# Routing order and the fetches of two expert slots in a fused attention and mixture-of-experts kernel

## The chip, the cores and the metric

The kernel runs on one core of one Trainium2 chip, as one program. The metric is device time in microseconds (us), and a kernel's time is the median of its runs. Lower is better.

The engines have the names that the profile gives them: PE is TensorE's matrix product and PEld its loading of weights, DVE is VectorE, ACT is ScalarE, POOL is GpSimd, and SP is SyncE, which here issues most of the transfers.

## The reference

Attention comes first, with two batches of 576 tokens, 8 heads and 64 columns a head. Its result, 1152 tokens of 512 values, goes through a top-1 mixture of 8 experts. An expert takes its tokens in their order up to a capacity of 288, and what comes after that is dropped (its row stays zero).

```python
q_rot, k_rot = rotate(q), rotate(k)
attn = softmax(q_rot @ k_rot.T / sqrt(D))
x = (attn @ v).transpose(0, 2, 1, 3).reshape(1152, 512)

logits = x @ w_gate                    # 8 experts
e = argmax(logits, 1)
gate = softmax(logits)[e]
...
h = maximum(disp[e] @ w1[e], 0)        # 512 -> 1024, up to 288 tokens
y = h @ w2[e]                          # 1024 -> 512
out[token] = gate[token] * y
```

The inputs are drawn at random, and q and k are scaled up by 5.76 and 5.75, so the tokens are spread unevenly over the experts. Worked out on the host with the reference, the first batch gives its experts 0, 0, 0, 18, 0, 452, 106 and 0 tokens, and both batches together 0, 33, 0, 18, 0, 454, 155 and 492.

## The kernel before

**Stages.** The attention works through eight steps, four pairs of heads for batch 0 and then four for batch 1, in an order written out by hand (`ORDER`). While batch 1 is worked on, the routing of batch 0 (`Router.batch(0)`, then `Router.first`) runs in between in small steps on DVE. `first` picks the expert with most tokens in batch 0; that is slot 0, with 288 tokens, and its weights are loaded and its tokens fetched while the attention goes on. It also picks the second expert of batch 0. The first four of slot 0's eight groups of the first product are made at the attention's end (until about 190 us in the trace).

**A slot** is one expert's work. `load` (L912, rows L920 and L923) brings eight tiles of weights, four of w1 and four of w2, on SP's queue. Each tile is split into a rounded high part on ACT (`split_hi`, L932) and a rest on DVE or POOL (`split_lo`, L936), since the matrix product takes rounded operands and three products are summed. `gather_tile` (L906) fetches up to 128 tokens by an indirect transfer on POOL's queue into the tile `xg`; `disp_t` (L950) transposes them on PE, and `disp_h` on ACT (L954) and `disp_l` on DVE (L958) write them to `d`, high part and rest. `gemm1_wide` (L1005) makes one of eight groups of the first product in 12 matmuls, `relu_hi` (ACT, L1030) and `relu_lo` (DVE, L1036 and L1037) put it into `h`. `gemm2` (L1101) makes the second product for 128 tokens in two steps of 12 matmuls or four of 6, `rows_a` (ACT, L1116) scales by the gate, and `scatter` (L1132) writes the rows out on POOL's queue. A slot of 64 tokens has forms of its own (`gemm1_few`, L1056; `ht_copy`, L1060; `ht_transpose`, L1071; `split_tok`, L1079 and L1084; `disp5_h` and `disp5_l`, L962 and L965).

**Buffers.** There are two sets of eight raw weight tiles, used by turns (`raw[0]` for slot 0), and one set of split tiles, so a tile can be split for the next slot only when the slot before has used it, and loaded for the slot after only when it has been split. `xg` is one buffer for all slots, and so are `d`, `d1` and `h`.

**Slot 0's plan.** `first_slot` follows the hand-written list `PLAN`, in which each entry is one step, emitted in that order on its engine (`manual_schedule`). G, RH, RL, M, YA, YD and YS are a group of gemm 1, relu high and rest, gemm 2 (M.2j and M.2j+1 are the two steps for the j-th 128 tokens), scaling, and scatter. SH and SL split slot 0's w2; VH and VL split slot 1's w1. DT, DH and DL transpose slot 1's tokens and write `d`. X fetches the tokens of the next slot, and E makes the register loads. B is one step of the second routing, which is interleaved here: `Router.batch(1)`, then `Router.finish`.

**The second routing.** `batch(1)` sums the logits (the small product LL is L547), finds each token's expert (OH, L572), counts with products (L587), and makes M (L645) and the table of tokens by expert (product L651, result `tab`, L658). Between its steps `order` (L744 to L795) sorts the experts: slot 0's is known, slot 1 is the second expert of batch 0, the rest go by their counts. `finish` (L802 and L806) selects all eight slots' rows of the table by that order, and `tables` (L670 to L687) turns them into the fetch indices `gi`, the scatter indices `si` and the gates. As soon as `gi` is there, slot 1's three tiles of tokens are fetched. Step X of the plan then fetches three tiles of the next slot into the same `xg`.

**The branch.** E.0 copies the 18 numbers of `order` to `after` (L1431), and E.1 loads registers from them. SP loads eight experts' numbers (L1434), and all five engines load eight numbers of the general path (L1436) and the flag (L1437). `If` (L1444) then takes the usual path when the slots' counts stay within `MOST`, here 160, 288, 64 and 64 tokens and none after that. `usual` is straight-line code for the four slots by the list `STEPS`, worked on in the order `SEQUENCE` (1, 3, 2, 4), where slot 2 has 288 tokens and slots 1, 3 and 4 have 160, 64 and 64; the entries have the slot behind the point and carry the letters above, with LD a load, SP a split on POOL, and C and T the copy and the transposition of a small slot. This part isn't bound to the order of the list: a scheduler moves instructions within it. The other path, `slots`, goes through the slots with a jump table each (`later_slot`, `ahead`).

## Time and profile before

| what | value |
|---|---|
| runs | 313.56, 314.19, 316.22 us |
| median | 314.19 us |
| the profiled execution: its own time | 315.87 us |
| its span (first to last instruction) | 314.1 us |
| mean granted clock of TensorE | 0.928 |
| busy: PE, PEld | 282.9 us (90%), 255.1 us (81%) |
| busy: DVE, ACT, POOL | 224.5 us (71%), 194.1 us (62%), 153.2 us (49%) |

A profile shows one execution. In its rows a line number is the line of the kernel that made the instruction, `out<-in` are the program's names for the tiles, and the granted clock is the share of full speed that TensorE was given. A busy share is a mean over stages with different limits: the attention (until 190 us) has DVE and PE both nearly full, the routing stage (190 to about 220) has a long chain of small DVE steps beside PE's work, and in the last 40 us little but PE's work is left. What an edit is worth has to be read in the stage that it touches.

### The profile page before, as it was taken

The page shows a single profiled execution, that of the slowest core. Times are in us where ns is not written, and L with a number is a line of the kernel's source. Part 1 is how long each engine was busy: PE and PEld are TensorE (multiplying, and loading weights), DVE is VectorE, ACT ScalarE, POOL GpSimd, SP SyncE. Part 2 cuts the span into 40 slices and gives each one's busy share as a digit, 9 for nine tenths or more (in the row PEclk, how much of TensorE's full clock was granted, in tenths as well). Part 3 has the DMA queues.
Part 4 walks back from the last instruction along what each step waited for, and adds up shares of the span by engine and source line. Part 5 has one row for each costly group of instructions (what it writes and reads, how often), then busy time and mean ns, then how long its engine had stood idle before and what let it go on. Part 6 is the DMA issues. An engine that isn't in the chain of part 4 may idle for free. (4 is left out here: it accounts for less than half of the span.)

```text
span 314.1 us, 5909 instructions
## 1 busy us (share of the span) xinstructions
PE 282.9 (90%) x1920; PEld 255.1 (81%) x1920; DVE 224.5 (71%) x475; ACT 194.1 (62%) x435; POOL 153.2 (49%) x197
## 2 busy tenths in 40 slices
PE   4699999999999988898999999997976995999990
PEld 2387999999999887897998999865974694998890
DVE  3989779789988999898977829973264548366511
ACT  1158779789888875477899943711435385356541
POOL 4999968959312877905316631166330064100251
PEclk9979999999999999589999999996975699799997
DMA  5576869675643764237987117725586489600020
GB/s 169 144 210 166 189 195 250 162 181 138 167 104 79 181 157 101 47 73 199 341 184 263 40 48 257 269 75 158 198 301 258 154 285 337 231 0 0 2 76 15
DMA packets 36103, 50.29 MB, mean 160 GB/s; under 512 B 10328, under 2 KB 20696, under 8 KB 36064
## 3 DMA queue, kind: packets, MB, share of 16 engines
q1 hardware_dynamic: 34608, 45.61, 49.5%
q0 software_dynamic: 1456, 4.22, 4.2%
q8 instruction: 17, 0.28, 0.4%
q14 instruction: 22, 0.18, 0.2%
HBM read 31.57 MB, written 6.49 MB: 121 GB/s over the span
## 5 line engine op out<-in xcount | busy, mean ns | idle before, releaser
L316 ACT ACTIVATE pe<-sc,mx 128x576 f32<-128x576 f32 x72 | 53.6, 746 | 12.5 <-DVE mx L307 11.8
L307 DVE TENSOR_REDUCE mx<-sc 128x1 f32<-128x576 f32 x72 | 53.8, 751 | 9.2 <-PE sc L303 5.5
L350 DVE TENSOR_TENSOR PTl<-pt,PTh 128x512 fp32r<-128x512 f32 (+1 forms) x80 | 48.8, 630 | 5.6 <-ACT PTh L346 5.1
L346 ACT CAST PTh<-pt 128x512 fp32r<-128x512 f32 (+1 forms) x80 | 42.1, 548 | 12.3 <-PE pt L328 9.9
L328 PE MATMUL pt<-cst,pe 128*128 128x128 f32 x288 | 43.9, 282 | 0.9 <-ACT pe L316 0.4
L303 PE MATMUL sc<-d,QS 128*128 128x288 f32 x224 | 43.9, 321 | 0.7 <-ACT pe L316 0.7
L1132 POOL DMA_INDIRECT out_dram<-y,si x10 | 11.2, 1115 | 61.4 <-DVE y L1125 35.8
L936 DVE TENSOR_TENSOR w2l<-raw,w2h 128x1024 fp32r<-128x1024 f32 x18 | 23.2, 1300 | 20.5 <-ACT w2h L932 20.3
L328 PEld LDWEIGHTS pt<-cst,pe 128*128 128x128 f32 x288 | 34.7, 145 | 3.4 <-ACT pe L316 1.0
L391 PE MATMUL acc<-PTh,VV 128*128 128x288 f32 x128 | 36.9, 311 | 0.2
L391 PE MATMUL acc<-PTl,VV 128*128 128x288 f32 x128 | 34.9, 295 | 0.0
L303 PEld LDWEIGHTS sc<-d,QS 128*128 128x128 f32 x224 | 33.2, 197 | 1.7 <-ACT pe L316 1.6
L1101 PE MATMUL sc<-w2h,h 128*128 128x512 f32 (+2 forms) x80 | 31.3, 436 | 2.6 <-DVE h L1037 2.6
L932 ACT CAST w2h<-raw 128x1024 fp32r<-128x1024 f32 x20 | 20.7, 1048 | 11.7 <-issue 6.3
L211 POOL TENSOR_TENSOR raw<-raw,cst 128x640 f32<-128x640 f32 (+1 forms) x16 | 23.2, 1449 | 6.9 <-PE pt L243 3.7
L1005 PE MATMUL sc<-d,w1h 128*128 128x288 f32 (+1 forms) x120 | 25.9, 314 | 0.0
L936 DVE TENSOR_TENSOR w1l<-raw,w1h 128x1024 fp32r<-128x1024 f32 x15 | 17.7, 1220 | 11.3 <-ACT w1h L932 11.3
L391 PEld LDWEIGHTS acc<-PTh,VV 128*128 128x128 f32 x128 | 24.2, 189 | 0.9 <-ACT accs L395 0.4
L906 POOL DMA_INDIRECT xg<-x_dram,gi x14 | 16.3, 1167 | 16.3 <-DVE h L1037 7.0
L391 PEld LDWEIGHTS acc<-PTl,VV 128*128 128x128 f32 x128 | 24.1, 188 | 0.0
L1101 PEld LDWEIGHTS sc<-w2h,h 128*128 128x128 f32 (+1 forms) x80 | 16.7, 209 | 7.7 <-ACT h L1030 3.3
L1101 PE MATMUL sc<-w2l,h 128*128 128x512 f32 (+2 forms) x56 | 22.2, 407 | 0.0
(235 smaller groups left out, 685.4 us busy)
## 6 DMA issues: line engine op xcount, KB each, us to landing
raw<-in_moe_w_dram SPq DMA_DIRECT2D x40, 512.0 KB, 5.8
d<-HH SPq DMA_DIRECT2D x28, 144.0 KB, 2.7
d<-LL SPq DMA_DIRECT2D x28, 144.0 KB, 2.4
out_dram<-raw SPq DMA_DIRECT2D x9, 256.0 KB, 3.0
raw<-in_k_dram SPq DMA_DIRECT2D x8, 256.0 KB, 3.0
raw<-in_q_dram SPq DMA_DIRECT2D x8, 256.0 KB, 2.8
raw<-in_v_dram SPq DMA_DIRECT2D x8, 256.0 KB, 3.0
x_dram<-xm SPq DMA_DIRECT2D x8, 256.0 KB
```

The source lines that it names most:

```text
L211: eng.tensor_tensor(R, x, cos.to_broadcast(full), ALU.mult)
L303: nc.tensor.matmul(o, st["QS", j][:, qc], st[k, j][:, cs], start=(x == 0), stop=(x == 1))
L307: self.nc.vector.tensor_reduce(mx, self.st[n]["sc", u][:, :, 0:288], AX.XY, ALU.max, negate=True)
L316: self.nc.scalar.activation(pe.rearrange("p (a c) -> p a c", a=2), st["sc", u][:, :, 0:288], AF.Exp, bias=st["mx", u], accum_out=self.sums ...
L328: nc.tensor.transpose(ps[:, c * P:(c + 1) * P], pe[:, 64 + c * P:64 + (c + 1) * P], self.ident)
L346: self.nc.scalar.copy(h, p)
L350: self.nc.vector.tensor_tensor(l, p, h.bitcast(F32), ALU.subtract)
L391: nc.tensor.matmul(acc[:, 0:288], w, m, start=(c == 1 and x == 0), stop=(c == 0))
L932: self.nc.scalar.copy(self.W[u][0], self.raw[q][u])
L936: eng.tensor_tensor(lo, self.raw[q][u], hi.bitcast(F32), ALU.subtract)
L1005: self.nc.tensor.matmul(ps[:, 0:n], w, self.d[:, c, a, 0:n], start=(c == 0 and x == 0), stop=(c == 3 and x == 2))
L1101: self.nc.tensor.matmul(o[0:r, 0:w], a, b, start=(c == 0 and x == 0), stop=(c == 7 and x == len(prods) - 1))
```

## The change

It has these parts.

- `first` also finds the third expert of batch 0. The second and third expert of batch 0 are slots 1 and 2, and their tables and fetches no longer need the sort. The usual path now holds when the slots have at most 160, 64, 288 and 64 tokens, and works on them in the order 1, 2, 3, 4.
- `slots12` selects the table rows of slots 1 and 2 alone, and slot 1's fetch has two tiles (`SECOND`: 128 and 32 tokens) in place of three. `order` runs behind that in steps O of the plan, and selects the rows of slots 3 and 4 at its end. The rows of slots 5 to 8, the kinds of the slots and the numbers of the jump tables are made in `others`, and the remaining tokens fetched in `whole`, both behind the branch on the general path.
- Before the branch one register, the flag, is loaded on every engine (L1467), and two experts' numbers on SP (L1471). The copy `after` is gone.
- Slot 2's weights are asked for in slot 0's plan (LDB), and its 64 tokens are fetched there in one tile (X.0). Slot 1's weights are asked for step by step (LDA). Slot 0's splits SG.7, VG.2 and VG.3 are on POOL.
- The step M.3 of slot 0's gemm 2 stands ahead of the transposes DT. Two groups of gemm 1 (G.7 and G.6) stand ahead of the routing's first product, and three small products of the routing that were on POOL (`val`, `jh`) are on DVE.
- Slot 4's tokens have a tile of their own, `xg4`.

The diff, cut:

```diff
     def batch(self, b, bank):
...
-        order = self.order() if b else iter(())
...
-        next(order, None)
...
-        G.tensor_tensor(val[:, :, 1], sm, keep, ALU.mult)
-        G.tensor_tensor(val[:, :, 0], self.const[:, C_PID + 5 * b:C_PID + 5 * b + 5], keep, ALU.mult)
+        V.tensor_tensor(val[:, :, 1], sm, keep, ALU.mult)
+        V.tensor_tensor(val[:, :, 0], self.const[:, C_PID + 5 * b:C_PID + 5 * b + 5], keep, ALU.mult)
...
-        G.tensor_tensor(jh, jh, val[:, :, None, :].to_broadcast([P, 5, 3, 2]), ALU.mult)
+        V.tensor_tensor(jh, jh, val[:, :, None, :].to_broadcast([P, 5, 3, 2]), ALU.mult)
...
     def first(self):
...
+        key3 = self.t("key3", [P, 8])
+        V.scalar_tensor_tensor(key3, self.f1, 32768.0, key2, ALU.mult, ALU.add)
+        V.tensor_reduce(km, key3, AX.X, ALU.min)
+        V.tensor_tensor(f2, key3, km.to_broadcast([P, 8]), ALU.is_equal)
+        V.tensor_tensor(fe, f2, self.e8, ALU.mult)
+        V.tensor_reduce(s, fe, AX.X, ALU.add)
+        V.tensor_copy(self.e0[:, 2:3], s)
+        self.f12 = self.t("f12", [P, 8])
+        V.scalar_tensor_tensor(self.f12, self.f1, 2.0, f2, ALU.mult, ALU.add)
...
+    def select(self, a, b):
+        V = self.nc.vector
+        tb = self.tb[:, 6 * a:6 * b]
+        big = [P, b - a, 6, 8]
+        tmp = self.ptb[:, 0:b - a]
+        V.tensor_tensor(tmp, self.tab[:, 1].rearrange("p (e w) -> p w e", w=6)[:, None].to_broadcast(big),
+                        self.perm[:, a:b, None, :].to_broadcast(big), ALU.mult)
+        yield
+        V.tensor_reduce(tb.rearrange("p (s w) -> p s w", w=6), tmp, AX.X, ALU.add)
+        yield
+        if a == 0:
+            yield from self.indices(self.slot_tables, tb, slice(0, 3 * b), self.fetch)
+        else:
+            yield from self.indices(self.slot_tables, tb, slice(3 * a, 3 * b))
...
-    def finish(self, fetch):
...
 PLAN = """
-SH.7 SH.5 SL.7 SL.5 B.0 B.1 B.2 G.4 RH.3 B.3 B.4 RH.0 B.5 B.6 B.7 B.8 B.9 RH.2 B.10 RL.0 RH.1 SH.4 B.11 B.12 RL.2 G.5
...
+G.7 RH.1 RH.2 RL.1 RH.0 SH.5 RL.0 B.0 G.6 B.2 RH.7 SH.4 SL.5 SH.7 B.1 G.5 B.3 B.4 B.5 B.7 RH.6 B.6 SG.7 RL.2 B.8 SH.6
...
+VH.3 O.12 O.11 YD.2 O.13 O.14 O.15 YS.2 LDB.0 M.3 YA.0 VG.3 LDB.2 LDB.1 DT.0 YS.0 YA.1 DT.1 DH.0 X.0 DH.1 DL.0 LDB.3
+DL.1 YS.1 LDB.4 LDB.6 LDB.7 LDB.5 E.0
...
-STRAIGHT = {1: 6, 2: 4, 3: 5, 4: 5}
-MOST = (160, 288, 64, 64, 0, 0, 0, 0)
-SEQUENCE = (1, 3, 2, 4)
+STRAIGHT = {1: 6, 2: 5, 3: 4, 4: 5}
+MOST = (160, 64, 288, 64, 0, 0, 0, 0)
+SEQUENCE = (1, 2, 3, 4)
...
+        self.xg4 = sp.tile([64, 1, DM], F32, name="xg4")
...
+            if name in ("LDA", "LDB"):
+                next(self.load(int(name == "LDA"), self.e1 if name == "LDA" else self.e2, (i,)))
...
             elif name == "X":
-                self.gather(self.tables[0], 3, 3)
+                self.gather_tile(self.tables[0], 3, i, 64)
+            elif name == "O":
+                next(order)
...
+    def flag():
+        moe.flag = nc.values_load(router.sei[0:1, 8:9], min_val=0, max_val=1, skip_runtime_bounds_check_because=why)
+        moe.ee = [None, None, None] + [expert(s) for s in (3, 4)]
...
-        for _ in moe.load(1, moe.e1):
-            pass
-        moe.first_slot(moe.t0, routing1(), registers())
+        moe.first_slot(moe.t0, routing1(), router.order(), flag)
```

How the instructions stand around the branch, before and after. On PE, from slot 0's last products to slot 1's first; `mp_...` and `sc` are PSUM banks, L1101 and L1122 are gemm 2, L950 and L971 the transposes of the fetched tokens. Before:

```order
L1101 MATMUL mp_2878<-w2l_2865,h 64x512
L950 MATMUL mp_2879<-cst,xg 128x128 x4
L950 MATMUL mp_2880<-cst,xg 128x128 x4
L950 MATMUL sc<-cst,xg 128x32 x4
L1101 MATMUL sc<-w2h_2862,h 128x512
...
L1101 MATMUL sc<-w2h_2864,h 128x512
L1436 TENSOR_LOAD after x8
L1437 TENSOR_LOAD after
L1444 COMPARE_AND_BRANCH
L1005 MATMUL sc<-d,w1h_70 128x160 x2
```

And after:

```order
L1122 MATMUL sc<-w2h_2873,h 128x512
...
L1122 MATMUL sc<-w2h_2875,h 128x512
L971 MATMUL mp_2891<-cst,xg 128x128 x4
L971 MATMUL mp_2892<-cst,xg 128x32 x4
L1467 TENSOR_LOAD sei
L1482 COMPARE_AND_BRANCH
L1026 MATMUL sc<-d,w1h_70 128x160 x2
```

The last half of gemm 2, which stood behind the transposes, stands ahead of them; there are two tiles of transposes, not three, and one register load, not nine.

On POOL, from the fetch of slot 1's tokens to the branch; L906 and L926 are the indirect fetches, L1132 and L1153 the scatters, L687 and L671 the gates' copy. Before:

```order
L637 TENSOR_TENSOR jh_3041<-jh_3041,val_3009 128x30
L906 DMA xg<-x_dram,gi_3116 128x512 x2
L906 DMA xg<-x_dram,gi_3116 32x512
...
L687 COPY gate_3118<-tb 128x24
L1132 DMA out_dram<-y_2867,si_2175 1152x512
L1132 DMA out_dram<-y_2869,si_2175 1152x512
L1132 DMA out_dram<-y_2868,si_2175 1152x512
L1436 TENSOR_LOAD after x8
L1437 TENSOR_LOAD after
L1444 COMPARE_AND_BRANCH
L1474 ISA
L906 DMA xg<-x_dram,gi_3116 64x512
```

And after (L956 is a rest of a weight split):

```order
L956 TENSOR_TENSOR w2l_2876<-raw_68,w2h_2875 128x1024
L956 TENSOR_TENSOR w1l_75<-raw_2_2863,w1h_74 128x1024
L926 DMA xg<-x_dram,gi_3085 128x512
L926 DMA xg<-x_dram,gi_3085 32x512
L671 COPY gate_3087<-tb 128x6 x2
L1153 DMA out_dram<-y_2881,si_2183 1152x512
L956 TENSOR_TENSOR w1l_77<-raw_3_2864,w1h_76 128x1024
L1153 DMA out_dram<-y_2879,si_2183 1152x512
L926 DMA xg<-x_dram,gi_3085 64x512
L1153 DMA out_dram<-y_2880,si_2183 1152x512
L1467 TENSOR_LOAD sei
L1482 COMPARE_AND_BRANCH
```

The fetch of the second slot's 64 tokens, which stood behind nine register loads and the branch, stands ahead of one, and three splits of weights are in POOL's list. (The three rows cut before are a second fetch of three tiles, whose tokens only the general path uses.)

On SP, around the branch of the changed kernel (`raw_68` and `raw_69` are the first set of weight tiles, `raw_0` to `raw_7` the second):

```order
L943 DMA raw_68<-in_moe_w_dram 128x2x512
L1467 TENSOR_LOAD sei
L1471 TENSOR_LOAD sei x2
L1482 COMPARE_AND_BRANCH
...
L940 DMA raw_3_2864<-in_moe_w_dram 128x1024
...
L940 DMA raw_69<-in_moe_w_dram 128x1024
```

The eight loads of the second slot, into the first set, now stand ahead of the branch; behind it come the loads of slots 3 (second set) and 4 (first set).

More of the change, by code (lines that the diff above doesn't have):

```diff
@@ L609, in batch @@
         V.tensor_reduce(pos, pr, AX.X, ALU.add)
-        next(order, None)
         yield
@@ L621, in batch @@
             V.tensor_tensor(pos, pos, off, ALU.subtract)
-        next(order, None)
         yield
@@ L640, in batch @@
         V.tensor_tensor(RR, self.iota[:, None, :].to_broadcast([P, 5, 128]), pos[:, :, None].to_broadcast([P, 5, 128]), ALU.is_equal)
-        next(order, None)
         yield
@@ L646, in batch @@
                         OH[:, :, :, None].to_broadcast([P, 5, 8, 6]), ALU.mult)
-        next(order, None)
         yield
@@ L652, in batch @@
         yield
-        for _ in order:
-            yield
         if b == 0:
@@ L673, in tables @@
         yield
-        if fetch:
-            fetch()
+        if tokens:
+            tokens()
             yield
-        g2 = self.t(f"sf{tag}", [P, n])
         V.tensor_scalar(g2, tv[:, :, 0], 0.5, 8192.0, ALU.is_lt, ALU.mult)
@@ L688, in tables, with new_tables @@
         yield
+    def new_tables(self, n, tag):
+        t = [self.t(f"{w}{tag}", [P, n], dt) for w, dt in (("gi", U32), ("si", U32), ("gate", F32), ("gf", F32), ("sf", F32))]
+        return t
     def first(self):
         V = self.nc.vector
+        s88 = [P, 8, 8]
         key = self.t("key0", [P, 8])
@@ L772, in order, with others @@
         V.tensor_reduce(se, tmp, AX.X, ALU.add)
         yield
+        more = self.t("more", [P, 8])
+        V.tensor_tensor(more, se[:, 1], self.usual, ALU.is_gt)
+        any_more = self.t("anymore", [P, 1])
+        V.tensor_reduce(any_more, more, AX.X, ALU.max)
+        self.sei = self.t("sei", [P, 9], I32)
+        V.tensor_copy(self.sei[:, 0:8], se[:, 0])
+        V.tensor_copy(self.sei[:, 8:9], any_more)
+        yield
+        yield from self.select(2, 4)
+    def others(self):
+        V = self.nc.vector
+        for _ in self.select(4, 8):
+            pass
+        cnt = self.se[:, 1]
+        nt = self.t("kinds", [P, 8])
+        V.tensor_scalar(nt, cnt, 0.0, None, ALU.is_gt)
+        for lim in LIMITS:
+            V.scalar_tensor_tensor(nt, cnt, float(lim), nt, ALU.is_gt, ALU.add)
@@ L880, in __init__ @@
         self.xT = cp.tile([P, 4, 64], F32, name="xT")
-        self.after = cp.tile([P, 2, 9], I32, name="after")
         self.early, self.pairs = [], []
@@ L1135, in scatter, with first_slot @@
         )
-    def first_slot(self, tables, routing, registers):
+    def first_slot(self, tables, routing, order, flag):
         V, G = self.nc.vector, self.nc.gpsimd
@@ L1172, in first_slot, with whole @@
             elif name == "DT":
-                pd[i] = self.disp_t(i, ROWS[i])
+                pd[i] = self.disp_t(i, SECOND[i])
             elif name == "DH":
-                self.disp_h(i, ROWS[i], pd[i])
-            elif name == "XH":
-                self.disp5_h(pd[i])
-            elif name == "XL":
-                self.disp5_l(pd[i])
-            elif name == "DL":
-                self.disp_l(i, ROWS[i], pd[i])
-        assert next(routing, None) is None
+                self.disp_h(i, SECOND[i], pd[i])
+            elif name == "DL":
+                self.disp_l(i, SECOND[i], pd[i])
+        assert next(routing, None) is None and next(order, None) is None
+    def whole(self):
+        self.nc.scalar.copy(self.d1[:, :, 0:64], self.d.bitcast(F32)[:, :, 0, 0:64])
+        self.nc.vector.tensor_copy(self.d1[:, :, 64:128], self.d.bitcast(F32)[:, :, 1, 0:64])
+        for j in (1, 2):
+            self.gather_tile(self.tables[0], 0, j, ROWS[j])
+            pr = self.disp_t(j, ROWS[j])
+            self.disp_h(j, ROWS[j], pr)
+            self.disp_l(j, ROWS[j], pr)
+        self.gather(self.tables[0], 3, 3)
     def slot(self, s, kind, nxt, tables, k):
@@ L1226, in slot, with ahead @@
                 self.rows(s, py[i], i, kind, tables, k + i, last if i == m else None)
-    def ahead(self, s, tiles):
-        if s <= NE:
-            self.gather(self.tables[0], 3 * (s - 1), tiles)
+    def ahead(self, s, nxt):
+        if s + 2 <= NE and (nxt or s == 1):
+            self.gather(self.tables[0], 3 * (s + 1), 3 if nxt == 3 or s == 1 else 1)
     def usual(self, ee):
@@ L1322, in later_slot @@
             arms = {4 * k + x: (5 if k == 1 else k, x) for k in range(5) for x in range(4)}
+        elif s == 2:
+            arms = {4 * k + x: (k, x) for k in range(5) for x in range(4)}
+            arms.update({20 + x: (5, x) for x in range(4)})
         else:
```

194 lines of the change are left out of this document (85 added, 109 removed).

## The prediction, made before the changed kernel was run

> **What bounds the kernel now.** I read the stages first, because TensorE is 90% busy on average and an average hides where it is not. This is the table of stretches, cut where TensorE's rows change; its columns are the stretch, its length, then busy time of PE, PEld, DVE, ACT and POOL, the granted clock, DMA share and GB/s.
>
> ```profile
> 210.70:215.20 4.50, 1.94 (x14) 1.33 (x12) 1.01 (x3) 0.68 (x1) 2.14 (x3) 0.87 0.40 123
> 215.20:220.40 5.20, 5.20 (x13) 4.07 (x13) 1.82 (x4) 1.52 (x4) 3.07 (x4) 0.50 0.82 219
> 220.40:227.20 6.80, 6.80 (x61) 6.77 (x59) 1.47 (x2) 3.29 (x4) 1.99 (x2) 0.97 0.52 200
> 227.20:229.80 2.60, 0.24 (x3) 0.10 (x2) 2.60 (x5) 1.68 (x4) 1.99 (x3) 1.00 0.43 66
> 229.80:237.20 7.40, 7.38 (x41) 7.33 (x41) 2.86 (x12) 1.57 (x6) 1.64 (x2) 0.59 1.00 390
> 237.20:242.60 5.40, 2.81 (x7) 1.70 (x6) 2.76 (x5) 3.84 (x5) 0.00 (x0) 0.50 0.62 247
> 242.60:248.20 5.60, 5.55 (x14) 3.61 (x15) 3.69 (x5) 1.28 (x2) 0.00 (x0) 0.51 0.08 11
> 248.20:263.80 15.60, 15.20 (x95) 12.58 (x93) 9.41 (x14) 12.30 (x21) 7.79 (x5) 1.00 0.86 318
> 263.80:267.20 3.40, 0.34 (x5) 0.32 (x4) 1.80 (x1) 0.00 (x0) 0.72 (x1) 1.00 1.04 342
> 267.20:272.00 4.80, 4.80 (x23) 4.59 (x22) 1.70 (x4) 2.16 (x4) 0.95 (x1) 0.65 0.95 352
> 272.00:306.80 34.80, 34.80 (x224) 30.98 (x222) 17.10 (x29) 17.56 (x30) 6.03 (x4) 1.00 0.06 19
> ```
>
> From 272 to 306.8 TensorE is full at full clock: that stage is bound by matmuls, and no edit here changes their number. Between 210.7 and 272 there are four holes, and behind each a stretch at about half clock, where a matmul takes twice as long. The loss of a stretch is its length minus (busy x clock): holes 2.8 (4.50 less 1.94 x 0.87), 2.4, 4.0 (5.40 less 2.81 x 0.50, so half hole, half clock) and 3.1; slow clock 2.6, 3.0, 2.8 and 1.7. Together **22.4 us**. Next, who ended the holes (TensorE's waits from 190 on: us in total, times, longest), and the chain that ended last (start, us):
>
> ```profile
> PE sc L950 <- DMA xg<-x_dram,gi: 3.9, 2, 3.1
> PE sc L1101 <- DVE h L1037: 2.6, 1, 2.6
> PE mp L950 <- DVE w2l L936: 2.4, 1, 2.4
> ```
> ```profile
> 230.83 7.85 DMA raw<-in_moe_w_dram
> ...
> 257.40 0.88 PE sc L950 x8
> ...
> 259.75 6.98 DMA xg<-x_dram,gi
> ...
> 276.16 4.76 PE mp L1005 x36
> ```
>
> Hole 1 (210.7) waits for slot 1's tokens, hole 4 (263.8) for slot 4's. Hole 3 ends with a rest of h, but in the chain h comes after a split on ScalarE, and that after the weight tile that landed at 230.83 + 7.85 = 238.7. Hole 2 is put down to DVE, but the transposes there read xg: it waits for the next slot's tokens, which POOL could fetch only after its register loads. Their rows (ns min/median/max, first and last start):
>
> ```profile
> L1436 PEldq TENSOR_LOAD <-after x8: 300/306/494, 214.7 to 217.7; - x8
> L1436 ACTq TENSOR_LOAD <-after x8: 274/282/552, 220.7 to 223.2; - x8
> L1436 POOLq TENSOR_LOAD <-after x8: 283/289/542, 221.4 to 224.3; - x8
> ```
>
> **The change, part by part.** *Register loads.* Nine become one on four engines, seventeen become three on SP. Eight loads are 8 x 0.28 = 2.3 us on ScalarE, where the idle 3.24 us ahead of 224.60 (below) shrinks to about 0.7. TensorE ran its own loads while queued matmuls covered them (214.7 to 218.1, all inside the stretch 215.2 to 220.4), so there they were free, and the one left lies under the wait priced as gap below.
>
> *Tokens of slot 1.* The sort no longer precedes the fetch. Does the fetch start earlier? The rows that carry its chain:
>
> ```profile
> 190.52 0.28 PE L547 MATMUL mp<-LL,cst 128*64 128x8 f32 x2
> 191.96 0.20 DVE L572 TENSOR_TENSOR OH<-iv,wv 128x40 bf16<-128x40 f32 x1
> 194.11 1.22 DVE L936 TENSOR_TENSOR w2l<-raw,w2h 128x1024 fp32r<-128x1024 f32 x1
> 204.63 0.18 DVE L672 CAST gi<-gf 128x24 uint32<-128x24 f32 x1
> 205.59 1.73 POOL L906 DMA_INDIRECT xg<-x_dram,gi  x1 [7.01 <-DVE h L1037]
> 207.62 1.97 POOL L906 DMA_INDIRECT xg<-x_dram,gi  x1 [0.31 <-issue]
> ```
>
> The new plan puts two groups of gemm 1 (12 matmuls each, 1.6 us, since 36 of that width took 4.76 above) ahead of the small product L547, so L547 runs 3.1 us later and OH, with one split of 1.2 now in between and a little slack taken out, near 195.5, 3.5 us later. From OH to gi took 12.7; out go some 25 sorting instructions (2.8 us) and two thirds of the selection (0.9), in comes one more split (1.2): gi near 205.3, and with a wait for the table's product near 206. So **the fetch starts no earlier**. What helps is that the last half of gemm 2 (M.3, 12 matmuls; 13 rows took 5.20 at 0.50, so 2.6 at full clock) now stands before the transposes: TensorE needs the tokens near 214.4 and not at 210.7. With landings of 4.0 to 7.0 us (next fence) after 206.2 and 208.2 they are there at 210 to 215. Hole 1 goes, and the slow M.3. In its place: a wait of 1.0 (0 to 1.5) near 202, where TensorE by the same count is through with its second block of gemm 2 one microsecond before M of the routing table is made, and a new gap, since M.3 no longer covers the copy of the transposed tokens. ScalarE first does the row scaling (0.69), then d (two in 1.08), DVE d's rest (0.69):
>
> ```profile
> 220.66 0.69 ACT L1116 ACTIVATE y<-sc,gate 128x512 f32<-128x512 f32 x1 [3.90 <-PE sc L1101]
> 224.60 2.94 ACT L932 CAST w2h<-raw 128x1024 fp32r<-128x1024 f32 x3 [3.24 <-issue]
> 215.41 1.08 ACT L954 CAST d<-mp 128x512 fp32r<-128x512 f32 x2
> 216.03 0.69 DVE L958 TENSOR_TENSOR d<-mp,d 128x512 fp32r<-128x512 f32 x1 [3.32 <-ACT d L954]
> DMA to landing us min/median/max: 4.0/5.5/7.0
> ```
>
> That chain is 0.2 (start of the scaling) + 0.69 + 0.6 + 0.7 = 2.2 from the end of M.3; eight transposes, 0.88 in the chain above, fill 0.9 of it: gap 1.3 (1.0 to 2.0, with and without the scaling's wait). One tile of transposes fewer gives back 0.8 (1.94 x 0.87 against 0.9).
>
> *Tokens of the second slot.* One fetch of 64 rows, issued before the branch, once the transposes of slot 1 have read the tile (near 215); landing 4 to 7 later, at 219 to 222. TensorE wants them three groups (five of them make the 6.80 above, so 3 x 1.35) after 216.6, at 220.7: with the median landing and half a microsecond to issue a wait of 0.5 (0 to 1.5) in place of hole 2. POOL's three new splits at 2.4 us each (255.18 below) stand before that fetch. The last should end near 214 and cost nothing then; if ScalarE's half of it came 2 us late, the fetch would too.
>
> *Weights of the second slot.* All eight are asked for in slot 0's plan; before, SP reached them only at 215.86, and a split-bound issue stopped it until 228:
>
> ```profile
> 215.86 1.04 SPq L923 DMA_DIRECT2D raw<-in_moe_w_dram  x2
> 228.12 0.37 SPq L923 DMA_DIRECT2D raw<-in_moe_w_dram  x1
> 255.18 2.42 POOL L936 TENSOR_TENSOR w2l<-raw,w2h 128x1024 fp32r<-128x1024 f32 x1 [0.85 <-ACT w2h L932]
> ```
>
> Hole 3 goes: the split that waited until 238.7 now finds its tile landed some 15 us ahead. But the same pattern returns one slot later: SP's list for slots 3 and 4 has a load for slot 4 in third place that waits until the second slot's split has read the tile, and two thirds of slot 3's w1 stand behind. I reckon slot 3's last w1 tile at 17 to 19 us after slot 1's gemm 1 ends, its split 2 us later, and TensorE ready for it 20 us after (slot 1's gemm 2, all of the second slot): 1.0 (0 to 6), the middle of that estimate; the 6 is hole 3 come back. Slot 4's tokens get a tile of their own and can be fetched at once: hole 4 goes.
>
> *Attention.* `first` gets seven small dependent DVE instructions, near 140, at about 0.2 each (1.4 us). DVE is the nearly full engine there; its idle pieces there are some tenths each, so I take half: 0.7 (0 to 1.4).
>
> *Clock.* The gap of 1.3 and the wait of 0.5 may start another slow stretch. The rows for how little is enough:
>
> ```profile
> 122.00:124.00 2.00, 0.99 (x9) 0.76 (x7) 1.97 (x4) 0.56 (x1) 1.92 (x2) 1.00 0.30 68
> 124.00:136.00 12.00, 10.89 (x55) 10.17 (x54) 10.81 (x25) 5.96 (x15) 8.84 (x11) 0.57 0.26 60
> ```
>
> Here 1.0 us idle was followed by 12 us at 0.57, and after 229.8 a hole of 2.4 by 0.59. One stretch costs 1.7 to 3.0 by the table; I take 2.0 (0 to 5.6, two of them), nearest to the 2.6 behind hole 1, which this gap succeeds in a smaller form. The Trainium skill (TensorE: Matmul & The Clock Gate, The HAM clock gate) says the clock falls only after an idle window of about 3.4 us. By that rule the gap would cost nothing and the estimate would be 2.0 lower; the holes of 2.4 and 1.0 us here speak against it.
>
> **The sum.** Gone 22.4 + 0.8; back 1.0 + 1.3 + 0.5 + 1.0 + 0.7 + 2.0 = 6.5. Net 16.7: the 315.87 of the profiled execution become 299.2. That execution lies 1.7 above the median of the runs (314.19), so a run should show **297.5 us**.
>
> **The rivals.** *Weights of slot 3 late (0.20).* SP's blocked order decides: if the last w1 tile lands 8 us after a delayed issue, TensorE waits 5 us and a slow stretch (1.7) follows: 303.5. For it: hole 3 was just that, 7.85 us in the chain. Against: eight loads fewer are left behind the branch.
>
> *Fetch under weight traffic (0.12).* Slot 1's fetch now runs beside eight prefetched tiles; before, the last of its traffic was over by then. At 259.75 a fetch under 1.04 share took 6.98. If both fetches queue up behind each other so, the second lands near 217, the next slot's near 223.5: 2 + 2 and one more slow stretch of 2.6, 304. The Trainium skill (DMA: Bandwidth & Descriptors, Issuing engines are not separate DMA queues) says that transfers of all issuers share the same 16 engines and interleave, which speaks against moving loads beside this fetch; the 6.98 agrees.
>
> *The clock stays low (0.05), the slower side.* Were the gap at 215 to 217 and the waits after it enough to hold 0.5 as from 231 to 248, each microsecond of matmul work costs another. TensorE's work after 216.6 is about 68 us; from 33 us at half clock on, the gain is gone. Held through slots 1, 2 and a third of slot 3, the time is 317. Against: at 248 the clock came back after 5 us of unbroken matmuls, and nothing that long is missing now.
>
> *The general branch is taken (0.03).* The usual branch holds only if the third expert of the first routing keeps at most 64 tokens. Worked out with the reference on its seeded inputs it has 18, and the others 155, 492 (capped at 288) and 33: it holds. If not, 8 register loads, some 25 small DVE steps at 0.2, a second fetch and slots without interleaving come on top: 330 or more.
>
> **How the numbers follow.** Forecast 0.60, with 293 to 301.5 of its own. All costs at their low ends (only the gap's 1.0 left) give 292.0, all at their high ends (18) 309; not all go wrong together, so the range is 291.5 to 306, which takes in both middle rivals. A measurement tells about 1% from no change: faster 0.92 (forecast and the first two rivals), within 1% 0.03 (the milder part of the clock rival), slower 0.05.
>
> **What would show it.** Right: no TensorE wait above 2 us between 205 and 265; slot 1's first 160-wide matmul near 217, its last group ended near 231; the 288-wide group starting near 253; ScalarE's idle before slot 1's first w2 split under 1 us. Wrong in part: a hole ended by w1 splits ahead of the 288-wide group, or by xg at the transposes. Wrong altogether: clock 0.5 past 240, or the second register load on every engine.

## The result, and the profile after

The changed kernel takes **303.67 us** (median of four runs, 301.63 to 304.35), against 315.21 before on the same chip: a ratio of 0.962, 95% interval 0.954 to 0.970. The prediction was 297.5 with a range of 291.5 to 306. The direction was right, and the time lies in the range, but only 11.5 us came where 16.7 were forecast. The profiled execution took 303.65, with a span of 301.9 and a mean clock of 0.975. The profile before is of an execution 1.7 us above its kernel's median, so 1.7 of what two profiles differ by here is no gain of the change.

The stages of the changed kernel (stretch, length, busy time of PE, PEld, DVE, ACT and POOL, granted clock, DMA share, GB/s):

```profile
200.40:201.80 1.40, 0.13 (x5) 0.04 (x3) 1.38 (x5) 1.24 (x2) 0.00 (x0) 1.00 1.02 404
201.80:206.60 4.80, 4.78 (x20) 3.24 (x20) 4.78 (x12) 2.00 (x3) 2.48 (x1) 1.00 1.05 414
206.60:209.50 2.90, 0.03 (x1) 0.00 (x0) 2.73 (x15) 0.00 (x0) 0.00 (x0) 1.00 1.02 414
209.50:210.70 1.20, 1.17 (x11) 1.17 (x11) 1.11 (x1) 0.00 (x0) 0.00 (x0) 1.00 1.05 408
210.70:215.10 4.40, 4.40 (x15) 3.43 (x15) 4.01 (x27) 0.00 (x0) 2.16 (x4) 0.61 0.95 350
215.10:222.40 7.30, 7.30 (x33) 5.58 (x32) 2.30 (x7) 2.31 (x3) 4.54 (x4) 1.00 0.12 34
222.40:224.80 2.40, 1.33 (x11) 0.92 (x9) 0.89 (x2) 2.02 (x4) 2.02 (x2) 1.00 0.66 169
224.80:228.70 3.90, 3.90 (x35) 3.90 (x35) 3.45 (x4) 3.21 (x4) 3.06 (x3) 1.00 0.61 220
228.70:236.00 7.30, 7.30 (x67) 7.15 (x66) 3.96 (x17) 3.26 (x9) 2.94 (x3) 1.00 0.32 91
```

The four holes of the kernel before are gone. From 224.8 on TensorE is full at full clock through slot 1's groups, where the kernel before had holes 2 and 3 and the half clock. What is new lies ahead of that: holes at 200.4 and 206.6, while DVE is full. TensorE's waits from 186 on, all that there are (us in total, times, longest):

```profile
PE mp L642 <- DVE M L637: 2.9, 1, 2.9
PE sc L1122 <- DVE of L594: 1.3, 1, 1.3
PE mp L1122 <- DVE h L1105: 0.8, 1, 0.8
PE sc L1026 <- ACT d L975: 0.7, 1, 0.7
PE sc L1026 <- DVE d L979: 0.4, 1, 0.4
```

L642 is the routing table's product (L651 in the kernel before). It starts 22.3 us after the attention's last logit product (L410); before, it took 15.9. The two marks before, and after:

```profile
184.55 1.01 PE L410 MATMUL pt<-fw,accs 128*128 128x72 f32 x8
200.48 1.21 PE L651 MATMUL sc<-M,RR 128*128 128x48 f32 x10
```
```profile
187.25 1.01 PE L410 MATMUL pt<-fw,accs 128*128 128x72 f32 x8
209.53 1.31 PE L642 MATMUL mp<-M,RR 128*128 128x48 f32 x10 [2.90 <-DVE M L637]
```

The forecast had put the wait for it at 1.0. DVE's rows in the chain ahead of it tell why, beside POOL's; the last row is that of `sm` before:

```profile
197.52 0.42 DVE L1057 SCALAR_TENSOR_TENSOR h<-sc,h 128x256 fp32r<-128x256 f32 x1
197.95 0.19 DVE L570 TENSOR_REDUCE iv<-eq 128x5 f32<-128x40 f32 x1
198.17 1.83 DVE L572 TENSOR_TENSOR OH<-iv,wv 128x40 bf16<-128x40 f32 x1
...
203.06 2.38 DVE L599 TENSOR_SCALAR sm<-sm 128x5 f32<-128x5 f32 x1
```
```profile
197.54 2.41 POOL L956 TENSOR_TENSOR w2l<-raw,w2h 128x1024 fp32r<-128x1024 f32 x1
202.94 2.48 POOL L956 TENSOR_TENSOR w1l<-raw,w1h 128x1024 fp32r<-128x1024 f32 x1 [2.98 <-ACT w1h L952]
```
```profile
195.24 0.16 DVE L599 TENSOR_SCALAR sm<-sm 128x5 f32<-128x5 f32 x1
```

OH took 0.20 before and takes 1.83; the same `sm` row took 0.16 and takes 2.38. Both are busy, not idle, and both end within 0.1 us of a split on POOL: 198.17 + 1.83 = 200.00 against 199.95, 203.06 + 2.38 = 205.44 against 205.42. These are SG.7 and VG.2, which the change moved to POOL. The rows between them tell that not every instruction is held: the rest of h, with one operand in PSUM, takes its usual 0.42 beside the split, and the reduction `iv` 0.19.

The span divided at two marks, the last logit product and slot 1's first 160-wide matmul:

| stretch | before | after | moved | forecast |
|---|---|---|---|---|
| to the last logit product (attention) | 184.55 | 187.25 | +2.7 | +0.7 |
| from there to slot 1's first group | 35.9 | 36.8 | +0.9 | -4.1 |
| from there to the end of the span | 93.7 | 77.8 | -15.9 | -13.3 |
| span | 314.1 | 301.9 | -12.2 | -16.7 |

The forecast's column comes from its 0.7 for the attention, its 217 for slot 1's first group and its 299.2 for the profiled execution, less 1.8 around the span.

### The profile page after: what moved, and what is told of

Same layout as the page of the kernel before. It is cut to its first block, busy times and chain, and to the rows that moved or that the text cites. A ratio compares the mean times of both kernels' runs of the same rounds, so it can differ in the third digit from the quotient of the medians.

```text
span 301.9 us, 5837 instructions
## 1 busy us (share of the span) xinstructions
PE 273.8 (91%) x1916; PEld 246.0 (81%) x1916; DVE 224.1 (74%) x475; ACT 193.9 (64%) x433; POOL 151.0 (50%) x193
## 5 line engine op out<-in xcount | busy, mean ns | idle before, releaser
L328 PE MATMUL pt<-cst,pe 128*128 128x128 f32 x288 | 42.9, 278 | 1.5 <-ACT pe L316 0.4
L1153 POOL DMA_INDIRECT out_dram<-y,si x10 | 10.6, 1061 | 54.9 <-ACT y L1137 33.1
L328 PEld LDWEIGHTS pt<-cst,pe 128*128 128x128 f32 x288 | 33.9, 142 | 4.4 <-ACT pe L316 1.4
L303 PEld LDWEIGHTS sc<-d,QS 128*128 128x128 f32 x224 | 32.3, 192 | 2.4 <-ACT pe L316 1.6
L956 DVE TENSOR_TENSOR w2l<-raw,w2h 128x1024 fp32r<-128x1024 f32 x17 | 20.4, 1221 | 11.8 <-ACT w2h L952 9.8
L1122 PE MATMUL sc<-w2h,h 128*128 128x512 f32 (+2 forms) x80 | 27.2, 385 | 1.3 <-DVE of L594 1.3
L430 POOL TENSOR_TENSOR lp<-xu,rs 128x32 f32<-128x32 f32 x16 | 3.9, 244 | 36.4 <-ACT xu L418 26.8
L1026 PE MATMUL sc<-d,w1h 128*128 128x288 f32 (+1 forms) x104 | 20.5, 292 | 1.2 <-ACT d L975 0.7
L232 POOL TENSOR_TENSOR VV<-raw,VV 128x640 fp32r<-128x640 f32 x8 | 12.8, 1600 | 17.6 <-DVE VV L228 13.3
L1122 PE MATMUL sc<-w2l,h 128*128 128x512 f32 (+2 forms) x56 | 20.8, 375 | 0.0
L258 ACT ACTIVATE HH<-pt 128x512 fp32r<-128x512 f32 (+2 forms) x25 | 12.3, 500 | 13.0 <-PE pt L247 12.5
```

Source lines behind the costliest of these rows:

```text
L303: nc.tensor.matmul(o, st["QS", j][:, qc], st[k, j][:, cs], start=(x == 0), stop=(x == 1))
L328: nc.tensor.transpose(ps[:, c * P:(c + 1) * P], pe[:, 64 + c * P:64 + (c + 1) * P], self.ident)
L956: eng.tensor_tensor(lo, self.raw[q][u], hi.bitcast(F32), ALU.subtract)
L1026: self.nc.tensor.matmul(ps[:, 0:n], w, self.d[:, c, a, 0:n], start=(c == 0 and x == 0), stop=(c == 3 and x == 2))
L1122: self.nc.tensor.matmul(o[0:r, 0:w], a, b, start=(c == 0 and x == 0), stop=(c == 7 and x == len(prods) - 1))
```

## The experiments

Theory: in the routing stage DVE's small instructions stand still while POOL works on a split. Rivals: the weight traffic (a DMA share of 1.02 to 1.05) slows DVE, or the small product L547, placed 3 us later, makes the chain long by itself.

### The first split ahead of the chain

```diff
-G.7 RH.1 RH.2 ... SL.5 SH.7 B.1 G.5 ... RH.6 B.6 SG.7 RL.2
+SH.7 SG.7 G.7 RH.1 RH.2 ... SL.5 B.1 G.5 ... RH.6 B.6 RL.2
```

> The changed kernel (303.67 us) with one move: slot 0's split SH.7 and its rest SG.7 on POOL stand at the start of the plan, so that POOL's 2.4 us fall before the routing's chain on DVE. Theory (DVE's small instructions stand still while POOL works on a split): the row OH L572, 1.83 us in the changed kernel, falls to about 0.2; the second split VG.2 still runs inside the chain and holds some other small DVE instruction for about 2 us; the table's product starts about 1.6 us earlier, 302 us in all. Rival (the long rows come from weight traffic at a share of 1.02 to 1.05 of the DMA engines): OH stays at 1.8 and the time at 303.7, since the traffic is the same.

300.78 us (298.37 to 305.43), ratio to before 0.959 (0.948 to 0.970). From the last logit product to the table's product it takes 20.65 us and not 22.28: 1.63 less, just what OH lost (1.83 less 0.20). The whole time fell by 2.9, but its executions overlap with the changed kernel's. The second split now holds another instruction, a product of two tiles in SBUF that took 0.16 in the changed kernel, again until the split ends (203.00):

```profile
200.63 2.38 DVE L614 TENSOR_TENSOR val<-cst,keep 128x5 f32<-128x5 f32 x1
...
200.59 2.41 POOL L956 TENSOR_TENSOR w1l<-raw,w1h 128x1024 fp32r<-128x1024 f32 x1 [5.45 <-ACT w1h L952]
```

The traffic is as before, so this speaks against that rival.

### The second split behind the fetch, and both moves

```diff
-... VL.0 B.27 LDA.1 M.0 VG.2 B.28 ... O.15 YS.2 LDB.0 ...
+... VL.0 B.27 LDA.1 M.0 B.28 ... O.15 VG.2 YS.2 LDB.0 ...
```

> The changed kernel with one move: the split VG.2 on POOL stands behind the fetch of slot 1's tokens and the tables, just ahead of the scatter YS.2. Theory (DVE held by POOL): the row sm L599, 2.38 us in the changed kernel, falls to about 0.2, OH stays near 1.8, the table's product starts about 2.2 us earlier, TensorE's wait of 2.9 us for M falls to about 1, about 301.5 us. Rival (weight traffic): sm stays at 2.4 and the time at 303.7. Second rival (TensorE's wait for M has another cause, the later product L547): the row shortens but the wait for M stays above 2.5, 303.5.

> Both moves of the two kernels before in one: no POOL split inside the routing's chain. Theory: OH and sm near 0.2, TensorE's two waits in the routing stage (1.29 and 2.90 in the changed kernel) fall from 4.2 to under 1, the half-clock stretch behind them (4.4 us at 0.61, 1.7 lost) goes with them: 298.5 to 300 us, 4 to 5 less than the changed kernel, and that is the greater part of what the prediction missed. Rival (traffic): 303.7. Second rival (later product L547 bounds the stage): waits stay above 2.5 in all, 302.5.

The first half came as expected: 20.06 us from mark to mark with the one move (2.22 less, the loss of `sm`) and 18.42 with both (3.86 less, the sum); the wait for M fell from 2.9 to 0.6 and 0.4. So the later L547 isn't what made that wait. It does make the chain longer: with both holds gone, 18.42 is still 2.5 more than the 15.9 before, where the prediction had L547 3.1 later. The times did not come as expected: 299.05 in one execution and 310.4 to 311.4 in three with the one move, 300.05 and 308.8 to 310.7 with both. The executions fall into two groups. The profiled execution of the kernel with both moves, stretch by stretch from its last part of gemm 2 on:

```profile
214.00:216.00 2.00, 0.75 (x5) 0.29 (x3) 1.93 (x5) 0.69 (x1) 1.01 (x1) 1.00 0.75 285
...
223.00:224.00 1.00, 1.00 (x8) 1.00 (x6) 1.00 (x2) 1.00 (x2) 0.74 (x1) 0.54 0.39 127
...
228.00:232.00 4.00, 4.00 (x20) 4.00 (x20) 1.20 (x5) 0.80 (x3) 1.58 (x2) 0.50 0.54 164
...
242.00:243.00 1.00, 1.00 (x4) 0.81 (x3) 1.00 (x2) 0.63 (x1) 0.00 (x0) 0.50 0.00 0
243.00:244.00 1.00, 1.00 (x5) 0.53 (x4) 1.00 (x2) 0.00 (x0) 0.00 (x0) 0.72 0.69 225
```

TensorE is never idle from 222 on and yet runs at 0.50 for 20 us, which costs 10. The full clock comes back 3 us after gemm 2, with 512 columns a matmul, has followed the 160-wide groups (at 240.59). The two holes ahead of the drop are the gap behind the transposes (0.71 + 0.35, from 219.8 to 221.1), known from the changed kernel, and a new one of 1.25 at 214.7. Its cause is the old one in a new place:

```profile
212.68 2.36 DVE L657 CAST gi<-gf 128x6 uint32<-128x6 f32 x1
...
215.14 0.74 DVE L1146 SCALAR_TENSOR_TENSOR y<-sc,gate,y 32x512 f32<-32x512 f32 x1
```
```profile
211.62 3.40 POOL L956 TENSOR_TENSOR w1l<-raw,w1h 128x1024 fp32r<-128x1024 f32 x1
```
```profile
215.94 0.50 PE L1122 MATMUL sc<-w2h,h 128*128 128x512 f32 x1 [1.25 <-DVE y L1146]
```

The split behind the fetch holds the cast of slots 3 and 4's indices, the scaling queued behind that comes late, and TensorE needs the bank that the scaling reads. POOL's own row has grown from 2.41 to 3.40: a split was running on DVE when it began (from 211.49 to 212.75), so the hold goes both ways.

### The split doubled

```diff
-... M.0 VG.2 B.28 ...
+... M.0 VG.2 VG.2 B.28 ...
```

> The changed kernel with the split VG.2 done twice on POOL, one behind the other (the second writes the same values again): nothing on the path reads the second one's result sooner. Theory: another small DVE instruction with two operands from SBUF or of the tensor_scalar kind is held for about 2.2 us in the 2.4 us of the second split, TensorE's wait for M grows from 2.9 to about 5, 306 us. Rival (weight traffic, or the chain's own length): POOL was idle there, so nothing moves, 303.7.

305.26 us (305.07 to 305.99). OH and `sm` are held as before (1.84 and 2.38), and a third instruction with them:

```profile
205.55 1.33 DVE L611 TENSOR_SCALAR keep<-pos 128x5 f32<-128x5 f32 x1
```

It took 0.15. Mark to mark it is 23.45 us, 1.17 more, which is that row's 1.18; the wait for M grew from 2.9 to 4.1. The size came out at half of the 2.2 expected, because the instructions between passed at their usual length (they have an operand in PSUM, or are a reduction or a reciprocal), and `keep` met only the second split's last part. The direction and the place are the theory's.

### Both rests off POOL's way

```diff
-... M.0 VG.2 B.28 ... O.15 YS.2 LDB.0 ...
+... M.0 B.28 ... O.15 VL.2 YS.2 LDB.0 ...
```

(with SH.7 and SG.7 at the start of the plan, as above)

> The changed kernel with SG.7 on POOL at the start of the plan and slot 1's rest of w1 tile 2 on DVE (VL.2, behind the scaling YD.2) in place of VG.2 on POOL. In the kernel with VG.2 behind the fetch the hold only moved: the second gi L657 stood 2.36 us beside the split, YD.2 came late and TensorE waited 1.25 for it; then the granted clock fell to 0.5 at about 223 and came back only at 244. Theory (holds by POOL): gi back to 0.2, the wait for y L1146 gone, TensorE's waits of the routing stage 0.5 in all. What the clock then does is open between two readings: if the drop needs two holes close together (1.25 and 1.1), it does not come and the time is 298 to 299.5; if the hole of 1.1 behind the transposes of slot 1's tokens is enough once the clock has been full up to there, it comes again and most executions take 308.

297.97 us: three executions at 296.87 to 298.13 and one at 308.7; the ratio to before, without that one, is 0.949 (0.945 to 0.953). The profiled one has the whole stage without a long hole or a slow stretch:

```profile
215.00:218.00 3.00, 1.93 (x14) 1.36 (x12) 0.89 (x2) 2.04 (x4) 2.66 (x2) 1.00 0.10 16
218.00:222.00 4.00, 4.00 (x36) 3.91 (x36) 3.58 (x4) 3.57 (x6) 3.26 (x3) 1.00 0.78 285
222.00:230.00 8.00, 8.00 (x69) 7.80 (x69) 4.47 (x17) 3.47 (x8) 3.75 (x4) 1.00 0.33 92
```

Slot 1's first group starts 31.4 us after the last logit product; the forecast's number for the changed kernel was 31.75. So the holds are what the forecast missed in that stage. That the whole time meets the forecast's 297.5 is partly luck: in this profile the rest of the kernel behind the stage is 2.6 shorter than was forecast.

Slot 1's first fetch is now issued at 207.40, beside weight loads (DMA share 1.01), and lands after 6.6 us; in the changed kernel the holds had put it off until that traffic was ending, and the one of its two fetches whose landing the profile has took 2.6.

### The transposes ahead of M.3

```diff
-... LDB.0 M.3 YA.0 VG.3 LDB.2 LDB.1 DT.0 YS.0 YA.1 DT.1 DH.0 X.0 DH.1 DL.0 ...
+... LDB.0 DT.0 DT.1 M.3 YA.0 VG.3 LDB.2 LDB.1 DH.0 YS.0 DH.1 X.0 YA.1 DL.0 ...
```

> The kernel with both rests off POOL, and DT.0 and DT.1 put ahead of M.3 again, with the copies DH ahead of the scaling YA.1, so that the last half of gemm 2 covers the copy of the transposed tokens. Theory (the gap behind the transposes, and holes near it, set off the half clock that lasts through slot 1's 160-wide groups): the gap of 1.1 falls to under 0.3, no half clock from 220 to 245 in any execution, 296.5 to 298.5. Rival (the half clock there is a matter of the execution, not of the gap): executions near 308 as before. Second rival (the fetched tokens land after 216, so that the transposes wait, as in the kernel before): a wait of 1 to 3 us for xg, 299 to 301.

> The kernel with both rests off POOL and the transposes of slot 1's tokens ahead of M.3, measured again with more executions. In the first measurement one execution took 384.7 with a clock of 0.65 from its start to its end, and the four others 296.2 to 300.5. Theory (the gap behind the transposes sets off the half clock of slot 1's groups): with the gap covered, no execution near 308, median 297 to 299, and no TensorE wait for d over 0.3 us. Rival (a matter of the execution): one or two of six near 308.

The first measurement gave 296.21 to 300.53 in four executions (and the one of 384.66, at a clock of 0.65 from start to end, which tells nothing of this kernel). The second gave 298.35 (297.19 to 304.95), ratio 0.953 (0.948 to 0.957). The gap for d is gone from the waits, and the transposes wait for the tokens in its place:

```profile
PE mp L971 <- DMA xg<-x_dram,gi: 1.0, 1, 1.0
...
PE mp L642 <- DVE M L637: 0.4, 1, 0.4
```

None of these ten executions stands near 308, against one of four with the gap left in, which is too few to tell the two readings apart; and two are at 304.7 and 305.0 with a clock of 0.95, so that a milder form is not excluded. The time is that of the kernel with both rests off POOL: a hole of 1.0 for another of 1.1, since slot 1's two fetches land 6.6 and 5.7 us after their issue at 208.84 and 210.18.

### Slot 2's weights behind the branch

```diff
-... YS.2 LDB.0 M.3 YA.0 VG.3 LDB.2 LDB.1 DT.0 ... LDB.3 DL.1 YS.1 LDB.4 LDB.6 LDB.7 LDB.5 E.0
+... YS.2 M.3 YA.0 VG.3 DT.0 ... DL.1 YS.1 E.0
-G4.1 SH6.1 G3.1 ...
+LD0.2 LD2.2 LD1.2 LD3.2 LD4.2 LD6.2 LD7.2 LD5.2 G4.1 SH6.1 G3.1 ...
```

> The changed kernel with the eight loads of slot 2's weights taken out of slot 0's plan and put at the head of the list behind the branch. The prediction's theory (hole 3 went because these tiles are asked for early): SP comes to them at about 216, the loads of slots 3 and 4 queue up behind them, a split waits for its tile again and TensorE loses 3 to 6 us: 307 to 309. Rival (hole 3 went because the new order of the slots and of SP's list leaves no blocked load ahead of the tiles): issued from 216 on, the tiles land by 232 at the latest, their first split comes at 236, and the DMA engines have nothing to do between 215 and 222 anyway: within 1 us of the changed kernel, 303 to 304.7.

312.42 us (309.16 to 314.68), ratio to before 0.994 (0.989 to 0.999): nearly the whole gain is lost, more than the theory expected, and by another way than it said. No split waits long for a tile. The loads now run beside slot 2's fetch, issued at 225.75, and TensorE waits for its tokens until 232.09. The landing of all fetches of tokens, the wait, and the stretches behind it:

```profile
DMA to landing us min/median/max: 2.8/5.5/7.6
```
```profile
232.09 0.46 PE L971 MATMUL sc<-cst,xg 64*128 64x64 f32 x4 [1.19 <-DMA xg<-x_dram,gi]
```
```profile
228.00:230.00 2.00, 2.00 (x20) 2.00 (x20) 2.00 (x3) 2.00 (x4) 1.39 (x3) 1.00 1.03 399
230.00:234.00 4.00, 2.81 (x25) 2.59 (x23) 3.13 (x9) 1.08 (x5) 3.39 (x3) 0.95 1.05 374
234.00:238.00 4.00, 4.00 (x21) 4.00 (x20) 0.95 (x6) 0.61 (x2) 0.26 (x1) 0.50 0.61 168
...
246.00:248.00 2.00, 2.00 (x7) 1.30 (x7) 2.00 (x2) 0.42 (x1) 0.00 (x0) 0.69 0.46 145
```

Slot 2's fetch lands after 6.3 us, with a DMA share of 1.04. In the changed kernel these weights had been asked for by 205.5; the share from 223.74, where that fetch is issued, to 228.8 was 0.67, and the tokens were there by 228.82. Here the wait itself is 1.2, but it follows the gap behind the transposes by 5 us, and the clock stays at 0.50 from 234 to about 247. That half clock costs 6.5 of the 8.7 lost. The rival (the order of the list alone) is out too.

### Slot 2's tokens behind the branch

```diff
-... DT.1 DH.0 X.0 DH.1 DL.0 ...
+... DT.1 DH.0 DH.1 DL.0 ...
-G4.1 SH6.1 G3.1 ...
+X0.2 G4.1 SH6.1 G3.1 ...
```

> The changed kernel with the fetch of slot 2's 64 tokens (X.0) behind the branch. In the changed kernel POOL issued it at 223.74, behind VG.3 and a scatter, and TensorE read it at 228.82 without a wait. Theory (hole 2 went because the fetch stands ahead of the register loads): now it follows the last scatter and the branch, at about 226.3, lands at 230 to 231, TensorE waits 1.5 to 2.5 at the transposes: 305 to 306, more where the clock falls. Rival (hole 2 went because one register load has taken the place of nine): with one load the fetch is issued within 1.3 us of the last scatter's issue, the wait is under 1, and the time within 1 us of 303.7.

303.29 us (300.25 to 304.82), ratio 0.961 (0.953 to 0.967), the changed kernel's time. The fetch is issued at 225.16, 1.4 later, and TensorE's transposes start at 228.89 without a wait. The rival holds: in this kernel the place ahead of the branch is worth nothing once nine register loads are one.

### One register load in the kernel before

```diff
-        for s in range(NE):
-            regs[1].append(nc.values_load(sei[0:1, 1, s:s + 1], ...))
-            regs[0].append(nc.values_load(sei[0:1, 0, s:s + 1], ...))
-        regs[0].append(nc.values_load(sei[0:1, 0, 8:9], ...))
+        regs[1].extend([None] + [expert(s) for s in (2, 3, 4)])
+        flag.append(nc.values_load(sei[0:1, 0, 8:9], ...))
```

> The kernel before with the register loads of the changed one and nothing else: the flag on every engine and three experts' numbers on SP ahead of the branch, the eight numbers of the general path and the other experts behind it, on the general path alone. Theory (POOL's and SP's loads made hole 2 and the late weights of hole 3): POOL fetches the second slot's tokens at about 223.9 and not at 226.2, hole 2 (2.4) falls under 1, SP comes to the next weights 3 to 5 us earlier, the half clock from 231 on is shorter or gone: 306 to 310. Rival (the loads were covered; the holes are made by the transfers themselves): 313 to 315.

309.55 us (307.80 to 312.15), ratio to before 0.990 (0.986 to 0.993), so 3 to 4 us. TensorE's longest waits in it, and SP's issues:

```profile
PE sc L1101 <- DVE h L1037: 6.9, 1, 6.9
PE sc L950 <- DMA xg<-x_dram,gi: 3.8, 2, 3.1
```
```profile
212.68 1.39 SPq L923 DMA_DIRECT2D raw<-in_moe_w_dram  x2
...
222.76 0.37 SPq L923 DMA_DIRECT2D raw<-in_moe_w_dram  x1
```

Hole 2 is gone, and the clock is full from 218 to 234, but hole 3 has grown from 2.6 to 6.9. SP reaches the weights 3.2 us sooner than before, and its blocked issue 5.4 sooner (222.76 for 228.12), and the wait ends 4.7 sooner (237.97 for 242.65), but TensorE is there 8.9 sooner (231.1 for 240.0). The register loads alone are about a third of the change's gain, and without slot 2's weights most of it is lost too, as the run with these weights behind the branch showed.

### M.3 ahead in the kernel before

```diff
-... VL.2 E.0 YA.0 DT.0 YA.2 DT.1 YD.2 DT.2 X.2 M.3 DH.2 ...
+... VL.2 E.0 M.3 YA.0 DT.0 YA.2 DT.1 YD.2 DT.2 X.2 DH.2 ...
```

> The kernel before with M.3 put ahead of the transposes DT.0 to DT.2 and nothing else. The prediction's theory (hole 1 is filled by M.3, and the slow stretch behind it goes): the wait of 2.4 for the first tile and 1.7 for the second shrink by the 2.6 us of M.3, a gap of 1.0 to 1.3 follows the transposes: 311 to 313. Rival (what TensorE wins in hole 1 it loses at hole 2, since the second slot's tokens are fetched no earlier): 313.5 to 315.

311.98 us (308.37 to 316.90), ratio 0.992 (0.988 to 0.996). Hole 1 is filled: there is no wait between 205 and 216. The copies behind the transposes then leave 2.1 us open, more than the 1.0 to 1.3 expected (there are three tiles here, and the scaling stands ahead), and the clock falls there and stays at 0.50 until about 245, so that much of hole 1's worth is lost again:

```profile
PE sc L1005 <- DVE d L958: 2.1, 1, 2.1
```
```profile
222.00:224.00 2.00, 2.00 (x12) 2.00 (x11) 1.59 (x2) 2.00 (x4) 1.70 (x2) 0.50 0.94 277
...
244.00:248.00 4.00, 4.00 (x17) 2.86 (x16) 1.87 (x2) 2.08 (x2) 0.00 (x0) 0.89 0.12 4
```

### Slot 4's tokens in the shared tile

```diff
-                self.gather_tile(self.tables[0], k, i, r, xg=self.xg4 if s == last else None)
+                self.gather_tile(self.tables[0], k, i, r)
```

> The changed kernel with slot 4's tokens fetched into the shared tile xg, as before the change. The prediction's theory (hole 4 went because of the tile of its own): the fetch waits for the transposes of slot 3's tokens again, TensorE waits 2 to 3 us for slot 4's tokens and loses 1.7 more to the clock: 307 to 308.5. Rival (hole 4 went with the new order of the slots: slot 3's first 128 tokens are transposed at 242 and slot 4's are wanted at 252): the fetch is issued at about 243, lands by 249, no wait: within 1 us of the changed kernel.

303.06 us (301.18 to 304.46), with no wait for xg. But the run does not tell what it was meant to: the list has slot 4's fetch ahead of slot 3's, and in a shared tile the later one writes over it, so that slot 4 works here on slot 3's first tokens, which land early. Whether a shared tile with the fetches in the other order would bring hole 4 back stays open.

## Why the prediction was right, and where it was short

**What bounded the kernel before** was read rightly. The four holes and their slow stretches were the loss, and from slot 1's first group to the end 15.9 us went, where 13.3 were forecast. Holes 1 and 2 went in the kernel before with the one edit that the prediction named for each; hole 4's cause was not told apart.

**Register loads: right.** Alone they give 3 to 4 us, and the wait passes on to the weights. The sum had no term for the loads alone; it took hole 2 and hole 3 out together.

**POOL's three splits: the step that failed.** The prediction said that the last "should end near 214 and cost nothing", looked only at what is queued behind them on POOL, and gave the other two no price. The last one ended at 222.2 and cost nothing all the same: the fetch behind it waited for the transposes, and DVE had nothing to do from 220 to 222. The two others held DVE for 1.63 and 2.22 us in the chain to the routing table, shown by taking out the one, the other and both: 1.63, 2.22 and 3.86 us. With both out the stage takes 31.4 us, against the 31.75 that follow from the forecast. The wait of 1.0 for the table was in truth 2.9, with 1.3 ahead of it, and 0.4 without the holds. It also fails the prediction's first sign of being right (no TensorE wait above 2 us between 205 and 265). The cover was missing because POOL's long instructions and DVE's short ones are not independent. The trace of before had it, at a place that the prediction did not look at: from 119 to 131 POOL works without a break, and there the first routing's `pos` and RR take 0.9 and 1.5, against 0.15 and 0.81 in the second routing.

```profile
123.33 0.91 DVE L632 SCALAR_TENSOR_TENSOR pos<-jt,pos 128x5 f32<-128x5 f32 x1
...
126.12 1.48 DVE L640 TENSOR_TENSOR RR<-cst,pos 128x640 f32<-128x640 f32 x1
```

The Trainium skill (SBUF — State Buffer, Who interferes with whom) states the rule: an instruction of DVE with two inputs in SBUF, or in a mode that uses both ports, and one of GpSimd that reads SBUF shut each other out for their whole length, and whichever started first is served. The traces agree: the held rows have two SBUF inputs (OH at 1.83, `val` at 2.38) or are casts and scalar operations in SBUF (`sm` at 2.38, `keep` at 1.33, the cast to `gi` at 2.36), and the rest of h from PSUM passed in 0.42.

**Slot 1's tokens: half right, with luck.** The fetch was not to start earlier than before (205.6), and it started at 212.6, later by the holds and by the attention's 2.7. (The prediction's own terms add up to 205.7 for `gi`, not 205.3; without the holds the fetch starts at 207.4, close to its 206.2.) It landed sooner than reckoned, in 2.6 us and not in 4 to 7, because the holds had put it off. Without them it takes the 6.6 of the prediction's rival of a fetch under weight traffic, and with the transposes ahead of M.3 TensorE waits 1.0 for it.

**The gap behind the transposes** was 1.1 for a forecast of 1.3. Of the signs that the prediction named, ScalarE's idle ahead of slot 1's first w2 split is 0.17 and not 3.24, and slot 1's groups start at 224.1 and not near 217, the 288-wide group at 256.4 and not near 253: 7 us late by the attention and the holds, then 3.4.

**Slot 2's tokens and slot 3's weights** were given 0.5 and 1.0 and cost nothing. The early weights matter, but not as the prediction argued: with them behind the branch no split waited long, and it was slot 2's fetch that came late beside them. That is the mechanism of the prediction's rival of a fetch under weight traffic, on another fetch than the one that it named.

**The attention** was given 0.7 for the new instructions of `first`, and differs by 2.7 in this pair of profiles. All of that is there before these instructions run: 1.25 us at 28 us already, where the code is the same, and 2.69 at the first routing's table product, which `first` follows. That product starts at 128.65 before and at 131.34 after, and TensorE's wait for it is 0.92 and 3.42. From there to the last logit product it takes 55.9 us in both, so the new instructions cost nothing that this pair shows. The wait differs from execution to execution (1.05 and 2.66 in two other profiles with the old `first`, 0.88 to 3.43 in nine with the new).

**The clock** cost 1.7 (4.4 us at 0.61) for a forecast of 2.0, but behind the wait for M and not behind the gap, so that the number agrees by luck. The rival that it stays low got 0.05 and did not come in the changed kernel. It did come in three of the experiments on it, at 6 to 12 us, so the mechanism is real; whether 0.05 was too little for the changed kernel, its four executions can't tell. What the prediction held against it, that the clock came back at 248 after 5 us of unbroken matmuls, was seen on 512-wide ones, and not on the 160-wide ones of slot 1.

## What to carry to other kernels

A long instruction on GpSimd is not free beside a chain of short VectorE instructions on SBUF: each one that meets it can wait out its whole length. Look for short instructions that are busy far beyond their usual time, since such a hold shows as busy time and in no list of waits. Removing a hole pays only as far as the next late arrival, and an edit that brings TensorE earlier should be followed to the next load that it can wait for. Where a stage comes out as forecast, look whether each step of it did: here a late fetch landed quickly because it was late.
